# A second V pair kept across two attention layers, parked in four PSUM banks, with a guarded return

## The chip, the cores and the metric

The kernel runs on one core of one Trainium2 chip. The metric is the device time of one execution in microseconds; it is about 1.7 us longer than the span from the first to the last instruction that the profile shows. Before the change the median of four runs measured with it was 187.67 us (187.57 to 188.01). A profile is one execution: that of the changed kernel was the slowest of its four (186.12 us), and those of "late_return", "deep_return" and "two_slots" were the slowest of theirs.

## The reference, cut to what matters

Four sub-layers act on a batch of four single tokens, in bf16: attention, a gated linear unit (GLU), the same attention again, the same GLU again. Weights and caches are the same both times.

```python
x = x + _A_ref(_layernorm(x), K, V, wq, wo)             # attention
x = x + _B_ref(_layernorm(x), w_gate, w_up, w_down)     # GLU
x = x + _A_ref(_layernorm(x), K, V, wq, wo)             # the same K, V, wq, wo
x = x + _B_ref(_layernorm(x), w_gate, w_up, w_down)
# attention: 4 sequences, 8 KV heads, 32 query heads of 128, the last 2048 positions
# D = 512, F = 1792
```

A K or V "pair" below is one KV head of two of the four sequences: 1 MiB, 8 KB per partition. There are 16 pairs of K and 16 of V.

## The kernel before

SBUF holds an arena of 50 slots of 4 KB per partition. K takes 32 of them and stays for both attentions. The other 18 are nine places of one pair each: wo takes four for both attentions, one V pair is kept from the first attention to the second, and about four places float. Everything else (V, wq, the GLU weights) streams through those and is read a second time for the second layer. The sync engine (SP) issues the loads in one order; each waits until the last reader of its place is done. So a place that frees late delays the load that will take it and every load after it.

```python
KEEP_V = cfg.get("KEEP_V", 1)
SB = (0, 1); PBS = (2, 3); OBS = (4, 5); WB = 6; CB = 7      # PSUM banks
...
def load_v(h, bp, k, n_use):
    load(("V", h, bp, k), n_use, "bw_8k", (2 * SLOT, pair_d(A_v, h, bp), True))
...
def q_proj(k, b0, b1):
    for n, i in enumerate((0, 1) if k == 0 else (1, 0)):     # two halves of q
        qb = OBS[n]
        for c in range(NC):
            ...                                              # 4 matmuls of 512 columns each
            P.op("tensor", "q%d_%d_%d" % (k, i, c), ..., r=tok(s) + [("xn",)], w=[("qrow", i)], banks=(qb,))
            done(name)                                       # frees the wq place after its last reader
        P.op("vector", "qt%d_%d" % (k, i), ...)              # transpose
        P.op("vector", "qc%d_%d" % (k, i), ...)              # scale
        P.op("tensor", "qs%d_%d" % (k, i), ...)              # spread over the partitions
        P.op("scalar", "qp%d_%d" % (k, i), ...)
...
all_v = [(h, bp) for h in range(HKV) for bp in range(2)]
keep = all_v[len(all_v) - KEEP_V:]
...                                                          # loads of the first attention
load_glu(0)
load_wq(1)
for h in range(HKV)[::-1]:                                   # second attention, heads 7 to 0
    for bp in range(2)[::-1]:
        if (h, bp) not in keep:
            load_v(h, bp, 1, 1)
load_glu(1)
```

A scheduler orders the operations of each engine from their dependences. "S2.0" and "S2.1" are the first two score blocks of the second attention.

Of the kernel before, what the change touches and what calls it, by code (L numbers as in the profile page):

```python
# [6 lines left out]
F32 = mybir.dt.float32  # L7
# [265 lines left out]
def build(nc, A_x, A_k, A_v, A_wq, A_wo, B_wg, B_wu, B_wd, out, cfg=None):  # L273
    cfg = dict(cfg or {})
# [1 line left out]
    tm.update(cfg.get("tm", {}))  # L276
    NS = cfg.get("NS", 50)
    GROUPS = cfg.get("GROUPS", [[0, 1, 2, 3]])
    KEEP_V = cfg.get("KEEP_V", 1)
    NG = len(GROUPS)  # L280
    assert GROUPS == [[0, 1, 2, 3]]
    N_DMA_SEMS = cfg.get("N_DMA_SEMS", 24)
# [32 lines left out]
    with es:  # L315
# [161 lines left out]
        def load_glu(k):  # L477
# [3 lines left out]
            for (a, b) in bounds_of(k):  # L481
                load(("wd", a, k), 1, "bw_8k", ((b - a) * D, wd_d[:, a:b, :], False))

        def load_v(h, bp, k, n_use):
            load(("V", h, bp, k), n_use, "bw_8k", (2 * SLOT, pair_d(A_v, h, bp), True))

# [101 lines left out]

        def q_proj(k, b0, b1):
            assert b0 == 0 and b1 == NB  # L590
            for n, i in enumerate((0, 1) if k == 0 else (1, 0)):
                qb = OBS[n]
                for c in range(NC):
                    name, o = wq_part(k, c, i)
                    s = need(name)

                    def e_q(pe, c=c, s=s, qb=qb, o=o):
                        last = None
                        for hh in range(4):
                            last = pe.matmul(ps[32 * hh:32 * hh + NB, qb, :], xn[:, c * NB:(c + 1) * NB],  # L600
                                             tile_ap(s)[:, o + hh * 512:o + (hh + 1) * 512],
                                             start=(c == 0), stop=(c == NC - 1))
                        return last
                    P.op("tensor", "q%d_%d_%d" % (k, i, c), 4 * tm["pe_row"], e_q,
                         r=tok(s) + [("xn",)], w=[("qrow", i)], banks=(qb,))
                    done(name)
                P.op("vector", "qt%d_%d" % (k, i), c_dve(512),
                     lambda v, qb=qb: v.transpose(  # L608
                         ebuf[:, :], ps[:, qb, :].rearrange("p (x k t) -> p x t k", k=32, t=2)),
                     r=[("qrow", i)], w=[("e", 0), ("e", 1)], banks=(qb,))  # L610
                qi = qh[:, i * 64:(i + 1) * 64]
                P.op("vector", "qc%d_%d" % (k, i), c_dve(64),
                     lambda v, qi=qi: v.tensor_scalar(
                         qi.rearrange("p (b c r) -> p b c r", c=4, r=REP),
                         ebuf[:, :].rearrange("p (r c y) -> p y c r", c=4, y=32)[:, 0:NB], SCALE, None, ALU.mult),
                     r=[("e", 0), ("e", 1)], w=[("qh", i)])

                def e_rep(pe, qi=qi):
                    last = None
                    for hh in range(4):  # L620
                        for a in range(4):
                            last = pe.matmul(ps[32 * a:32 * a + 32, CB, hh * 64:(hh + 1) * 64],
                                             ident_b[:, 32 * hh:32 * hh + 32], qi, start=True, stop=True)
                    return last
                P.op("tensor", "qs%d_%d" % (k, i), 300.0, e_rep, r=[("qh", i), ("ident_b",)],
                     w=[("cb",)], banks=(CB,))
                P.op("scalar", "qp%d_%d" % (k, i), c_act(256),
                     lambda a, i=i: a.copy(qrep[:, i * 256:(i + 1) * 256], ps[:, CB, 0:256]),  # L628
                     r=[("cb",)], w=[("qrep", i)], banks=(CB,))
# [144 lines left out]
        def attn(L):  # L774
            hs = list(range(HKV)) if L == 0 else list(range(HKV))[::-1]

            def front(ui):
                h = hs[ui]
                if L == 0:
                    k_transpose(h)  # L780
                k2 = softmax_unit("%d.%d" % (L, ui), h)
                if L == 2:
                    for bp in range(2):
                        pool.release(4 * h + 2 * bp)
                    fill()
                return k2

            ks = {}
            for ui in range(2):
                ks[ui] = front(ui)  # L790
                turn_p("%d.%d" % (L, ui), ks[ui])
            for ui, h in enumerate(hs):
                tag = "%d.%d" % (L, ui)
                if ui + 2 < HKV:
                    ks[ui + 2] = front(ui + 2)
                ov = pv_unit(tag, h, ks[ui], v_tiles[(L, h)])
                if ui + 2 < HKV:
                    turn_p("%d.%d" % (L, ui + 2), ks[ui + 2])
                wo_unit(tag, h, ov, ks[ui], ui == 0, ui == HKV - 1)
            P.op("vector", "xa%d" % L, tm["dve_fix"] + 40.0,  # L800
                 lambda v: v.tensor_tensor(xT[:, 0:NX], ps[:, WB, 0:NX], xT[:, 0:NX], ALU.add),
                 r=[("psw",)] + [("xT", b) for b in range(NB)], w=[("xT", b) for b in range(NB)], banks=(WB,))

        def glu(k, b0, b1, last=False):
# [7 lines left out]
            for n, nm in enumerate(("wg", "wu")):  # L812
                for c in range(NC):
                    name = (nm, c // 2, k)
                    s = need(name)

                    def e_g(pe, c=c, s=s, n=n):
                        last = None
                        for g in range(4):
                            o = c % 2 * F + g * NF  # L820
                            last = pe.matmul(ps[32 * g:32 * g + NB, SB[n], 0:NF], xn[:, c * NB:(c + 1) * NB],  # L821
                                             tile_ap(s)[:, o:o + NF], start=(c == 0), stop=(c == NC - 1))
                        return last
                    P.op("tensor", "gl%s%d_%d" % (nm, k, c), 4 * tm["pe_row"], e_g,
                         r=tok(s) + [("xn",)], w=[("gu", n)], banks=(SB[n],))
                    done(name)
                P.op("vector", "gt%s%d" % (nm, k), c_dve(NF),
                     lambda v, n=n: v.transpose(ebuf[:, 0:NF],  # L828
                                                ps[:, SB[n], 0:NF].rearrange("p (x k) -> p k x", k=NFC)),
                     r=[("gu", n)], w=[("e", 0), ("e", 1)], banks=(SB[n],))  # L830

                if n == 0:
                    P.op("scalar", "gex%d" % k, c_act(NH),
# [79 lines left out]

        all_v = [(h, bp) for h in range(HKV) for bp in range(2)]
        keep = all_v[len(all_v) - KEEP_V:]
        load_wq(0)
        for h in range(2):
            loads.append((("K", h), lambda _, h=h: load_k(h)))
# [6 lines left out]
                load_v(h, bp, 0, 2 if (h, bp) in keep else 1)  # L925
        load_glu(0)
        load_wq(1)
        v_tiles = {}
        for h in range(HKV)[::-1]:
            v_tiles[(0, h)] = [(bp, ("V", h, bp, 0)) for bp in range(2)]  # L930
            v_tiles[(2, h)] = [(bp, ("V", h, bp, 0 if (h, bp) in keep else 1)) for bp in range(2)[::-1]]
            for bp in range(2)[::-1]:
                if (h, bp) not in keep:
                    load_v(h, bp, 1, 1)
# [82 lines left out]
```

## Time and profile before

| | before |
|---|---|
| span of the profile | 186.2 us |
| HBM read | 72.88 MB |
| V loads of 1 MiB | 31 |
| DVE busy | 84.5 us |
| landing of the last load (second w_down) | 182.69 us |
| tail from there to the end | 3.53 us |

These are lines of the profile page of the kernel before: the clock granted to PE, the busy share of the 16 DMA engines and the rate, in 40 equal slices of the span; then the bytes; then the chain of waits that ended last, by engine.

```profile
span 186.2 us, 4414 instructions
...
PEclk9999997685857558576576555555796969955587
DMA  5999999999999999999999999999999999999970
GB/s 191 424 424 431 424 402 388 415 422 417 405 392 422 417 422 400 396 422 419 388 408 414 406 402 390 362 400 419 422 419 419 415 419 421 417 412 404 413 318 15
...
HBM read 72.88 MB, written 0.00 MB: 391 GB/s over the span
...
DMA 54%; PE 24%; SPq 14%; DVE 3%; ACT 2%; issue 2%; POOL 0%
```

The DMA row is at 9 nearly throughout, 54% of the chain is DMA, and the fullest slices run at 419 to 431 GB/s.

The next view is the table of windows for the start of the second attention. Columns: window, its length, then for each engine busy us and instructions, then PE's granted clock, the mean DMA load in units of 16 engines, and GB/s.

```profile
129.00:131.50 2.50, 2.50 (x28) 0.82 (x28) 0.62 (x3) 0.86 (x4) 0.00 (x0) 0.50 1.02 423
131.50:134.00 2.50, 1.98 (x22) 0.55 (x16) 2.09 (x7) 1.16 (x5) 0.03 (x1) 0.68 1.01 423
134.00:136.50 2.50, 2.50 (x39) 1.02 (x39) 1.40 (x8) 1.54 (x4) 0.99 (x5) 1.00 1.01 419
```

The stream runs at 419 to 423 GB/s there. By the landings of single loads, the V loads that land there follow each other by 2.48 to 2.49 us.

The timeline of DVE (the vector engine) around the end of the first attention and around the first half of q (start us, us, engine, line, operation, output and input; in brackets how long the engine was idle before, and what ended that):

```profile
107.32 0.20 DVE L749 TENSOR_TENSOR onb<-ps,rinv 128x16 bf16<-128x16 f32 x1 [4.79 <-PE ps L741]
...
126.55 0.72 DVE L608 STREAM_TRANSPOSE ebuf<-ps 128x512 f32<-128x512 f32 x1 [3.58 <-PE ps L600]
```

DVE is idle for 4.79 us before 107.32, which is room for four transposes. Second, SP's timeline between 128.5 and 134 us, which shows how many V loads were issued in that window:

```profile
129.09 4.93 SPq L382 DMA_DIRECT2D arena<-in_A_v_cache_dram  x2
```

Two: one at 129.09, the other ending at 134.02. Third, PE's timeline at the start of the second attention (L668 are the score blocks S2.0 and S2.1, L600 the last eight products of q):

```profile
128.99 3.84 PE L668 MATMUL ps<-arena,qbd 128*16 128x512 bf16 x32
132.59 0.86 PE L600 MATMUL ps<-arena,xn 128*4 128x512 bf16 x8
```

### The profile page before, as it was taken

The numbers are of one execution on the slowest core, as the hardware profiler recorded it, in microseconds if no ns is written. First come the engines' busy times: TensorE is split into PE (matmuls) and PEld (weight loads), VectorE is DVE, ScalarE is ACT, GpSimd is POOL, SyncE is SP. The second block draws the span as 40 slices with busy tenths as digits, with TensorE's granted clock in tenths as the row PEclk, the third lists the DMA queues.
The fourth block names the chain that finished last, engine by engine and source line by source line (L and its number), as shares of the span: only waits on it lengthen the run. The fifth ranks groups of instructions, "written<-read, shape, count | busy, mean of one in ns | idle before, by whom it ended". The sixth has DMA issues, their size and how long they took to land.

```text
span 186.2 us, 4414 instructions
## 1 busy us (share of the span) xinstructions
PE 101.8 (55%) x1944; PEld 55.3 (30%) x1944; DVE 84.5 (45%) x213; ACT 35.9 (19%) x100; POOL 14.9 (8%) x77
## 2 busy tenths in 40 slices
PE   0532423743616346252464545337899899947545
PEld 0101000332302223032233430311256565547112
DVE  5209998476582656727430031213754343312210
ACT  2003022330303003020020001002564332310100
POOL 4000010110101001010010000000121101120000
PEclk9999997685857558576576555555796969955587
DMA  5999999999999999999999999999999999999970
GB/s 191 424 424 431 424 402 388 415 422 417 405 392 422 417 422 400 396 422 419 388 408 414 406 402 390 362 400 419 422 419 419 415 419 421 417 412 404 413 318 15
DMA packets 15523, 73.17 MB, mean 393 GB/s; under 512 B 1160, under 2 KB 5264, under 8 KB 8720
## 3 DMA queue, kind: packets, MB, share of 16 engines
q1 hardware_dynamic: 15496, 72.88, 97.1%
q8 instruction: 15, 0.25, 0.5%
q14 instruction: 4, 0.03, 0.0%
q10 hardware_dynamic: 8, 0.00, 0.0%
HBM read 72.88 MB, written 0.00 MB: 391 GB/s over the span
## 4 chain that ended last, share of the span: by engine, by line
DMA 54%; PE 24%; SPq 14%; DVE 3%; ACT 2%; issue 2%; POOL 0%
DMA arena<-in_A_v_cache_dram 36%; SPq L382 14%; DMA arena<-in_B_w_down_dram 14%; PE ps L668 11%; PE ps L741 6%; DMA arena<-in_A_wq_dram 5%; PE ps L874 2%; PE ps L765 1%; ACT prow L685 1%; PE ps L697 1%; DVE nmax L676 1%; PE ps L898 1%; PE ps L720 1%; PE ps L600 1%; PE ps L821 1%
## 5 line engine op out<-in xcount | busy, mean ns | idle before, releaser
L741 PE MATMUL ps<-ebuf,arena 128*128 128x8 bf16 x1024 | 30.8, 167 | 30.8 <-DMA arena<-in_A_v_cache_dram 27.3
L668 PE MATMUL ps<-arena,qbd 128*16 128x512 bf16 x256 | 32.2, 628 | 15.7 <-DVE qbd L639 8.2
L741 PEld LDWEIGHTS ps<-ebuf,arena 128*128 128x128 bf16 x1024 | 28.6, 100 | 37.4 <-DMA arena<-in_A_v_cache_dram 33.4
L649 DVE STREAM_TRANSPOSE arena<-arena 128x1024 f32<-128x1024 f32 x32 | 37.9, 1218 | 3.6 <-DMA arena<-in_A_k_cache_dram 3.3
L676 DVE TENSOR_REDUCE nmax<-ps 128x1 f32<-128x512 f32 x16 | 11.0, 686 | 23.7 <-PE ps L668 23.7
L685 ACT ACTIVATE prow<-ps,nmax 128x512 bf16<-128x512 f32 x16 | 11.0, 687 | 37.9 <-DVE nmax L682 25.2
L642 ACT COPY qbd<-qrep 32x64 bf16<-32x64 bf16 x32 | 7.7, 242 | 41.2 <-PE ps L668 40.7
L668 PEld LDWEIGHTS ps<-arena,qbd 128*16 128x16 bf16 x256 | 6.4, 98 | 30.3 <-issue 21.6
L749 DVE TENSOR_TENSOR onb<-ps,rinv 128x16 bf16<-128x16 f32 x16 | 3.0, 186 | 26.5 <-PE ps L741 26.4
L710 POOL CAST s<-psm 128x1 bf16<-128x1 f32 x16 | 3.0, 188 | 143.2 <-ACT prow L685 143.2
L600 PE MATMUL ps<-arena,xn 128*4 128x512 bf16 x64 | 8.0, 596 | 7.3 <-DMA arena<-in_A_wq_dram 4.4
L702 ACT CAST prow<-ps 128x512 bf16<-128x512 f32 x16 | 9.4, 588 | 7.1 <-PE ps L697 7.0
L765 PE MATMUL ps<-onb,arena 128*128 128x4 bf16 x256 | 9.0, 165 | 3.1 <-DVE onb L749 3.1
L706 DVE STREAM_TRANSPOSE ebuf<-prow 128x256 f32<-128x256 f32 x16 | 7.0, 440 | 7.3 <-ACT prow L702 7.1
L821 PE MATMUL ps<-arena,xn 128*4 128x448 bf16 x64 | 6.6, 536 | 5.7 <-DVE xn L582 3.1
L765 PEld LDWEIGHTS ps<-onb,arena 128*128 128x128 bf16 x256 | 7.9, 100 | 3.7 <-DVE onb L749 2.8
L697 PE MATMUL ps<-prow,perm 64*128 64x256 bf16 x64 | 6.7, 291 | 2.3 <-ACT prow L685 2.1
L608 DVE STREAM_TRANSPOSE ebuf<-ps 128x512 f32<-128x512 f32 x4 | 2.9, 717 | 10.6 <-PE ps L600 10.5
L571 ACT ACTIVATE lnv<-lnv 128x4 f32<-128x4 f32 x4 | 0.8, 205 | 34.1 <-DVE lnv L568 34.1
L828 DVE STREAM_TRANSPOSE ebuf<-ps 128x448 f32<-128x448 f32 x4 | 2.6, 650 | 9.5 <-PE ps L821 9.5
L639 DVE COPY qbd<-qrep 32x64 bf16<-32x64 bf16 x32 | 5.3, 165 | 1.5 <-ACT qrep L628 0.9
L720 PE MATMUL ps<-sel_b,s 128*128 128x16 bf16 x48 | 3.8, 176 | 3.4 <-POOL s L714 2.6
(59 smaller groups left out, 65.1 us busy)
## 6 DMA issues: line engine op xcount, KB each, us to landing
arena<-in_A_v_cache_dram SPq DMA_DIRECT2D x31, 1024.0 KB, 17.0
arena<-in_A_k_cache_dram SPq DMA_DIRECT2D x16, 1024.0 KB, 16.1
arena<-in_A_wq_dram SPq DMA_DIRECT2D x8, 1024.0 KB, 9.1
arena<-in_A_wo_dram SPq DMA_DIRECT2D x4, 1024.0 KB, 24.3
arena<-in_B_w_gate_dram SPq DMA_DIRECT2D x4, 896.0 KB, 19.8
arena<-in_B_w_up_dram SPq DMA_DIRECT2D x4, 896.0 KB, 16.1
arena<-in_B_w_down_dram SPq DMA_DIRECT2D x2, 1024.0 KB, 12.7
arena<-in_B_w_down_dram SPq DMA_DIRECT2D x1, 768.0 KB, 6.9
```

Of the source, the lines that this page charges most:

```text
L382: o = P.op("sync", name, 0.0, lambda e, dst=dst, src=src: e.dma_start(dst, src), r=r, w=w, dma_bytes=nbytes, dma_rate=tm[rate])
L600: last = pe.matmul(ps[32 * hh:32 * hh + NB, qb, :], xn[:, c * NB:(c + 1) * NB], tile_ap(s)[:, o + hh * 512:o + (hh + 1) * 512], start=(c = ...
L642: P.op("scalar", "qe%s_%d" % (tag, a), c_act(64), lambda s_, dst=dst, src=src: s_.copy(dst, src), r=rd, w=[("q", k2, a)])
L649: P.op("vector", "T%d_%d" % (h, t), c_dve(1024), lambda v, v32=v32: v.transpose(v32, v32), r=[("slot", 4 * h + t)], w=[("slot", 4 * h + t)])
L668: last = pe.matmul(ps[32 * gi:32 * gi + NR, bank, :], qbd[:, q0:q0 + NR], kt[:, cp // 2, cp % 2, b % 2, :, :], start=(cp == 0), stop=(cp = ...
L676: lambda v: v.tensor_reduce(nmax[:, k2:k2 + 1], ps[:, bank, :], AXX, ALU.max),
L685: lambda a: a.activation(prow[:, :].rearrange("p (m x t) -> p m x t", x=16, t=2), ps[:, bank, :].rearrange("p (m t x) -> p m x t", x=16, t ...
L697: last = pe.matmul(ps[:, PBS[i], 0:256], perm[64 * i:64 * i + 64, jh * 128:(jh + 1) * 128], prow[64 * i:64 * i + 64, jh * 256:(jh + 1) * 2 ...
L702: lambda a: a.copy(prow[:, :].rearrange("p (y i t) -> p i y t", i=2, t=2), ps[:, PBS[0]:PBS[0] + 2, 0:256].rearrange("p i (y t) -> p i y t ...
L741: last = pe.matmul(ps[:, ob, bp * 8:bp * 8 + 8], src[:, j * 128:(j + 1) * 128], ev[:, j % 2, j % 16 // 2, x0:x0 + 8], start=(j == 0), stop ...
L765: last = pe.matmul(ps[:, WB, c * NB:(c + 1) * NB], tile_ap(s)[:, o + r_ * D + c * 128:o + r_ * D + (c + 1) * 128], ov[:, r_ * NB:(r_ + 1) ...
L821: last = pe.matmul(ps[32 * g:32 * g + NB, SB[n], 0:NF], xn[:, c * NB:(c + 1) * NB], tile_ap(s)[:, o:o + NF], start=(c == 0), stop=(c == NC ...
```

## The change

The intent is to keep a second V pair, V(head 7, pair 0), so that its second 1 MiB read is never made. The arena of 50 slots has no place to spare, so at the end of the first attention DVE moves the pair into PSUM banks 0 to 3 with four transposes ("st"), and moves it back into a freed SBUF place with four more ("us") when the second attention needs it. Transposing twice is meant to restore every bit. The kernel declares its PSUM tensor as 128 x 8 x 512 f32, so one of the eight bank numbers stands for 2 KB per partition, and four hold exactly the 8 KB per partition of a pair.

The banks must not be used in between, so gate and up products move from SB to OBS. Two guards order the return: the fourth transpose back waits for the scaling of the first half of q ("qc"), and the second half of q waits until the first half is spread ("qs"). The diff, cut (index changes of the GLU banks shortened):

```diff
-    KEEP_V = cfg.get("KEEP_V", 1)
+    KEEP_V = cfg.get("KEEP_V", 2)
...
+        STASH = SB + PBS
+        after_q = []
+        def stash(name):
+            s = need(name)
+            for n, b in enumerate(STASH):
+                src = tile_ap(s)[:, n * 1024:(n + 1) * 1024].bitcast(F32)
+                P.op("vector", "st%d" % n, ..., lambda v, src=src, b=b: v.transpose(ps[:, b, :], src),
+                     r=tok(s), w=[("stash", n)], banks=(b,))
+            done(name)
+        def load_stash(name):
+            left[name] = 1
+            def emit(s):
+                for n, b in enumerate(STASH):
+                    dst = tile_ap(s)[:, n * 1024:(n + 1) * 1024].bitcast(F32)
+                    o = P.op("vector", "us%d" % n, ..., lambda v, dst=dst, b=b: v.transpose(dst, ps[:, b, :]),
+                             r=[("stash", n)], w=[("slot", s + n // 2)], banks=(b,))
+                    o.prio += 60
+                    if n == 3:
+                        after_q.append(o)
+            loads.append((name, emit))
...
 # q_proj
+            qs = []
-                         r=tok(s) + [("xn",)], w=[("qrow", i)], banks=(qb,))
+                         r=tok(s) + [("xn",)], w=[("qrow", i)], banks=(qb,), after=qs if k else ())
...
+                while after_q:
+                    after_q.pop().deps.add(qc)
...
+                qs.append(qs_)
...
 # attention, after the last score block of the first layer
+                if L == 0 and ui == HKV - 1:
+                    stash(stashed)
...
 # GLU: gate and up products in OBS[n] instead of SB[n]
...
 # list of loads of the second layer
         load_wq(1)
+        load_stash(("V",) + keep[0] + (1,))
```

One thing moves that the diff does not spell out. Of the 16 products of q's second half, the first eight run ahead of S2.0 in both kernels. Before, PE ran S2.1 ahead of the last eight; after, the scheduler puts these between S2.0 and S2.1. PE's timeline after (L697 are the score blocks, L626 the products of q):

```profile
129.15 2.01 PE L697 MATMUL ps<-arena,qbd 128*16 128x512 bf16 x16
130.94 0.66 PE L626 MATMUL ps<-arena,xn 128*4 128x512 bf16 x8
131.39 2.09 PE L697 MATMUL ps<-arena,qbd 128*16 128x512 bf16 x16
```

More of the change, by code (lines that the diff above doesn't have):

```diff
@@ L482, in load_glu @@
                 load(("wd", a, k), 1, "bw_8k", ((b - a) * D, wd_d[:, a:b, :], False))
+        STASH = SB + PBS
[4 more added lines that the diff above has]
+                src = tile_ap(s)[:, n * 1024:(n + 1) * 1024].bitcast(F32)
+                P.op("vector", "st%d" % n, c_dve(512), lambda v, src=src, b=b: v.transpose(ps[:, b, :], src),
+                     r=tok(s), w=[("stash", n)], banks=(b,))
[5 more added lines that the diff above has]
+                    dst = tile_ap(s)[:, n * 1024:(n + 1) * 1024].bitcast(F32)
+                    o = P.op("vector", "us%d" % n, c_dve(512), lambda v, dst=dst, b=b: v.transpose(dst, ps[:, b, :]),
+                             r=[("stash", n)], w=[("slot", s + n // 2)], banks=(b,))
[3 more added lines that the diff above has]
+            loads.append((name, emit))
         def load_v(h, bp, k, n_use):
@@ L611, in q_proj @@
                 qi = qh[:, i * 64:(i + 1) * 64]
-                P.op("vector", "qc%d_%d" % (k, i), c_dve(64),
+                qc = P.op("vector", "qc%d_%d" % (k, i), c_dve(64),
                      lambda v, qi=qi: v.tensor_scalar(
@@ L624, in e_rep @@
                     return last
-                P.op("tensor", "qs%d_%d" % (k, i), 300.0, e_rep, r=[("qh", i), ("ident_b",)],
+                qs_ = P.op("tensor", "qs%d_%d" % (k, i), 300.0, e_rep, r=[("qh", i), ("ident_b",)],
                      w=[("cb",)], banks=(CB,))
+                qs.append(qs_)
                 P.op("scalar", "qp%d_%d" % (k, i), c_act(256),
@@ L820, in e_g @@
                             o = c % 2 * F + g * NF
-                            last = pe.matmul(ps[32 * g:32 * g + NB, SB[n], 0:NF], xn[:, c * NB:(c + 1) * NB],
+                            last = pe.matmul(ps[32 * g:32 * g + NB, OBS[n], 0:NF], xn[:, c * NB:(c + 1) * NB],
                                              tile_ap(s)[:, o:o + NF], start=(c == 0), stop=(c == NC - 1))
@@ L824, in glu @@
                     P.op("tensor", "gl%s%d_%d" % (nm, k, c), 4 * tm["pe_row"], e_g,
-                         r=tok(s) + [("xn",)], w=[("gu", n)], banks=(SB[n],))
+                         r=tok(s) + [("xn",)], w=[("gu", n)], banks=(OBS[n],))
                     done(name)
@@ L828, in glu @@
                      lambda v, n=n: v.transpose(ebuf[:, 0:NF],
-                                                ps[:, SB[n], 0:NF].rearrange("p (x k) -> p k x", k=NFC)),
-                     r=[("gu", n)], w=[("e", 0), ("e", 1)], banks=(SB[n],))
+                                                ps[:, OBS[n], 0:NF].rearrange("p (x k) -> p k x", k=NFC)),
+                     r=[("gu", n)], w=[("e", 0), ("e", 1)], banks=(OBS[n],))
                 if n == 0:
@@ L915, in build @@
         keep = all_v[len(all_v) - KEEP_V:]
+        stashed = ("V",) + keep[0] + (0,)
         load_wq(0)
@@ L930, in build @@
             v_tiles[(0, h)] = [(bp, ("V", h, bp, 0)) for bp in range(2)]
-            v_tiles[(2, h)] = [(bp, ("V", h, bp, 0 if (h, bp) in keep else 1)) for bp in range(2)[::-1]]
+            v_tiles[(2, h)] = [(bp, ("V", h, bp, 0 if (h, bp) in keep[1:] else 1)) for bp in range(2)[::-1]]
             for bp in range(2)[::-1]:
```

## The prediction

> **What bounds the kernel now.** The input stream. The page shows 72.88 MB read and the DMA row at 9 tenths in all but the first and the last two slices. In the chain that ended last DMA has 54%, waits before issues 14%, PE 24%. [...] the table of windows shows 419 GB/s for 129 to 161 us[...]. By each load's landing in the trace, consecutive 1 MiB V loads land 2.48 to 2.50 us apart. After the last w_down piece (182.69 us) 3.5 us of tail remain.
>
> **What the change does.**
> - It removes one 1 MiB load, the second read of V(head 7, pair 0): issued at 124.19 us, landed at 133.23 us, 2.48 us after the load before. Estimate: 2.48 us of stream.
> - It adds eight 512-element DVE transposes. Estimate 0.6 to 0.72 us each (0.72 us measured out of a PSUM bank; 1.22 us for 1024 elements in place), 5.5 us in all; DVE is 45% busy.
> - The four going out fit between that pair's landing (103.72 us) and DVE's next work at 107.32 us: estimate 103.8 to 106.7 us. They hold back the second w_up load from 104.8 to about 106.7 us, with 6 us of earlier loads still to land (7.8 now): nothing lost.
> - Of the four coming back, three start when two q products end (124.15 us) and take to 126.4 us; the q transpose starts at 126.55 us now and slips by 0 to 0.2 us. The fourth runs while PE and ScalarE spread q (127.6 to 128.4 us).
> - Gate and up products only change banks. PE puts the second half of q between the first two score blocks, so the second block's softmax comes about 1 us later. That attention is compute-paced to about 161 us, but the loads behind it land last: off the path.
>
> **Does the stream stay full?** The returned pair takes a free slot that a load would have had. At the issues of V(6,1), V(6,0), V(5,1) the stream today has 6.0 to 6.2 us left to land; I expect 3.1 to 3.7. The smallest backlog today is 2.96 us (first w_down piece, 112.2 us); 106 to 129 us ran at 394 GB/s. So a loss of 0 to 0.4 us is possible, no drained queue. After 134 us score blocks free the K slots and the queue is deep again.
>
> **How much is on the path.** Everything after the removed load lands 2.5 us earlier: last landing near 180.2 us, the same tail. 187.68 - 2.48 + 0.1 = 185.3 us, 1.3% faster, inside the 2% band. Range 184.7 to 186.4. Chances: faster by over 2% 0.03, within 2% 0.95, slower by over 2% 0.02.
>
> **What the profile would show.** HBM read 71.83 MB; 30 V loads, not 31; DMA row still at 9; DVE busy about 90 us; landings as before up to the last wq load (130.75 us, within 0.3 us); the first score block of the second layer near 129 us, at most 0.3 us late; the last landing 2.5 us earlier, then the same 3.5 us; a w_down landing still the chain's last DMA piece.
>
> **What would make it wrong.** A bubble of 1 us or more in the stream between 130 and 140 us from the thinner backlog; transposes into PSUM slower than 0.9 us, so that the end of the first attention, and the layer change with it, slips; slow packets on wq or V loads falling differently; a lower granted PE clock that delays slot releases.

## The result

| | before | after |
|---|---|---|
| time, median of 4 runs (range) | 187.67 us (187.57 to 188.01) | 185.49 us (185.17 to 186.12) |
| span of the profile | 186.2 us | 184.4 us |
| HBM read | 72.88 MB | 71.83 MB |
| V loads | 31 | 30 |
| DVE busy | 84.5 us | 89.5 us |
| last landing | 182.69 us | 181.75 us |
| tail after it | 3.53 us | 2.64 us |

The ratio is 0.9885 (95% interval 0.9855 to 0.9915). All ratios here are the mean time of one kernel's runs over that of the other's of the same rounds, so not quite the ratio of the medians quoted. Executions over 1.5% slower than the fastest of the same kernel are left out of the means. The changed kernel is 1.15% faster, inside the 2% band, and its time is within 0.2 us of the prediction. But the last two rows are not what the prediction said: the last landing came only 0.94 us earlier, and the tail shrank.

The same lines of the page, after:

```profile
span 184.4 us, 4421 instructions
...
PEclk9999995585766756755555555555897897885569
DMA  5999999999999999999999999999999999999980
GB/s 198 425 427 427 425 403 391 411 421 419 409 387 425 419 421 403 392 419 419 400 391 414 412 407 393 403 350 417 330 396 419 419 423 416 418 416 402 412 341 24
...
HBM read 71.83 MB, written 0.00 MB: 390 GB/s over the span
...
DMA 52%; PE 25%; SPq 16%; DVE 4%; issue 2%; ACT 0%
```

The DMA row still says 9, yet the rate has two holes, 350 and 330 GB/s. A slice is 184.4/40 = 4.6 us. The first hole is the slice from 120 us, in the wq loads; the kernel before has one there too (362). The second, from 129 to 134 us, is new: that part of the page before has 419 and more. The table of windows, cut finer, tells better:

```profile
129.00:131.50 2.50, 2.50 (x32) 0.89 (x32) 0.63 (x3) 0.84 (x5) 0.00 (x0) 0.72 1.12 349
131.50:134.00 2.50, 2.16 (x38) 0.82 (x30) 2.06 (x7) 1.13 (x4) 0.06 (x1) 1.00 0.87 321
134.00:136.50 2.50, 2.34 (x23) 0.51 (x23) 1.51 (x7) 1.22 (x4) 0.70 (x4) 1.00 1.01 370
```

Beside 423, 423 and 419 GB/s before. In the first window the engines were busier than usual (1.12) and moved less. The packets explain that: an 8 KB packet usually takes 311 ns, and between 128.8 and 136.3 us 18 of them took 1.0 to 2.03 us. A stalled packet counts as a busy engine in this view (a share of 1.12 at 349 GB/s, against 1.02 at 423 before), so the rate shows the loss and the share does not.

DVE's timeline, after:

```profile
103.59 2.50 DVE L492 STREAM_TRANSPOSE ps<-arena 128x512 f32<-128x512 f32 x4 [1.21 <-DMA arena<-in_A_v_cache_dram]
107.16 0.19 DVE L778 TENSOR_TENSOR onb<-ps,rinv 128x16 bf16<-128x16 f32 x1 [1.06 <-PE ps L770]
...
124.18 1.91 DVE L502 STREAM_TRANSPOSE arena<-ps 128x512 f32<-128x512 f32 x3 [1.34 <-PE ps L626]
126.70 0.72 DVE L634 STREAM_TRANSPOSE ebuf<-ps 128x512 f32<-128x512 f32 x1 [0.61 <-PE ps L626]
127.45 0.22 DVE L639 TENSOR_SCALAR qh<-ebuf 128x64 bf16<-128x64 f32 x1
127.71 0.72 DVE L502 STREAM_TRANSPOSE arena<-ps 128x512 f32<-128x512 f32 x1
```

The moves are as planned: about 0.62 us each going out, in the idle time at 103.6 to 106.1, with DVE's next operation even a little earlier (107.16 against 107.32); three back, then the q transpose 0.15 us later than before (126.70 against 126.55), and the fourth right after the scaling. DVE was idle before the first two groups and again before its next work, so none of its own work waits for them in this view.

SP, in the same window as before:

```profile
129.23 4.91 SPq L382 DMA_DIRECT2D arena<-in_A_v_cache_dram  x5
```

Five issues instead of two. One of them is V(5,1), that is head 5, pair 1, which was issued at 133.49 before and at 131.65 after, because the last products of q run before S2.1 and the wq place is free earlier: they end at 133.45 before and 131.60 after, each time 0.05 us before the issue.

### Where the 1.83 us of the profile came from

The last landing alone misleads. The trace keeps 16 semaphore increments at different times for each load of the stream. The author read each as the landing of one DMA engine's share, since the page counts 16 engines; the trace does not name the engine, so "the slowest engine" below means the last of a load's 16 increments. Read so, each load has 16 landings; their spread over a load grows here from 1.50 us (before) and 1.76 (after) at the last wq load to 2.88 and 3.29 at the end. Three numbers add up to the span: the mean of the 16 landings of the last w_down load, how far the slowest engine is behind that mean (lag), and the tail after it.

| us | mean landing | lag | tail | sum = span |
|---|---|---|---|---|
| before | 181.25 | 1.44 | 3.53 | 186.22 |
| after | 179.79 | 1.97 | 2.64 | 184.39 (sum 184.40) |
| change | -1.46 | +0.53 | -0.89 | -1.83 |

So of about 2.5 us of stream that were removed, 1.46 reached the mean landing, the slowest engine gave back 0.53, and a shorter tail added 0.89.

A second measure isolates the stretch of V loads: from the mean landing of the last wq load to that of the last V load. Before, 15 loads took 37.83 us, 2.522 each. In "after", 14 loads should take 35.31 and took 36.50: 1.2 us lost. This is the "loss" in the tables below.

### The tail

PE's timeline at the end; the products with w_down are L874 before and L905 after.

```profile
180.86 3.15 PE L874 MATMUL ps<-arena,hT 128*4 128x256 bf16 x28 [1.93 <-DMA arena<-in_B_w_down_dram]
```

```profile
179.93 1.04 PE L905 MATMUL ps<-arena,hT 128*4 128x256 bf16 x16 [1.09 <-DMA arena<-in_B_w_down_dram]
181.17 1.01 PE L905 MATMUL ps<-arena,hT 128*4 128x256 bf16 x12 [0.20 <-DMA arena<-in_B_w_down_dram]
```

Before, 28 products took 3.15 us without a gap: at half clock, PE could not keep up with the pieces of w_down as they landed. After, they took 2.05 us and PE waited for the pieces. The windows just before and during them, before and then after:

```profile
177.50:180.90 3.40, 0.83 (x14) 0.15 (x12) 0.87 (x2) 0.00 (x0) 0.00 (x0) 0.99 0.83 333
180.90:184.30 3.40, 3.11 (x28) 1.63 (x28) 0.25 (x1) 0.25 (x1) 0.00 (x0) 0.50 0.13 51
```

```profile
174.70:178.20 3.50, 2.84 (x32) 1.10 (x33) 0.82 (x2) 0.43 (x3) 0.00 (x0) 0.50 1.01 408
178.20:181.60 3.40, 2.12 (x36) 1.16 (x31) 0.87 (x2) 0.34 (x2) 0.00 (x0) 1.00 0.33 130
```

The column before the DMA share is the clock: 0.50 during the products before, 1.00 after. In the clock records of the two traces it is either 1.00 or 0.50, and every entry but the last lasts 3.41 us or a multiple of it. In this pair of windows the lower clock came after the lesser PE work: before, the window with PE busy for 0.83 us was followed by half clock; after, the one with 2.84 by full clock. But PE's busy time does not decide it alone. With the records of these two traces cut into steps of 3.41 us, a step in which PE was busy for less than 1.25 us was followed by half clock in 25 of 25 cases, and one at half clock with over 3.25 us busy by full clock in 8 of 8; yet after 3 of 9 steps at full clock with over 3.25 us busy the clock fell to half. What decides there, no run tests.

### The profile page after: what moved, and what is told of

Read it like the earlier page. It is cut to its first block, busy times and chain, and to the rows that moved or that the text cites. A ratio compares the mean times of both kernels' runs of the same rounds, so it can differ in the third digit from the quotient of the medians.

```text
span 184.4 us, 4421 instructions
## 1 busy us (share of the span) xinstructions
PE 101.2 (55%) x1944; PEld 54.7 (30%) x1944; DVE 89.5 (49%) x221; ACT 35.7 (19%) x100; POOL 14.8 (8%) x77
## 3 DMA queue, kind: packets, MB, share of 16 engines
HBM read 71.83 MB, written 0.00 MB: 390 GB/s over the span
## 4 chain that ended last, share of the span: by engine, by line
DMA 52%; PE 25%; SPq 16%; DVE 4%; issue 2%; ACT 0%
DMA arena<-in_A_v_cache_dram 33%; SPq L382 16%; PE ps L697 11%; DMA arena<-in_B_w_down_dram 9%; PE ps L770 8%; DMA arena<-in_A_wq_dram 5%; DMA arena<-in_B_w_up_dram 5%; PE ps L726 2%; PE ps L794 1%; DVE ps L492 1%; PE ps L626 1%; DVE nmax L705 1%; PE ps L749 1%; PE ps L905 1%; PE ps L852 1%
## 5 line engine op out<-in xcount | busy, mean ns | idle before, releaser
L697 PE MATMUL ps<-arena,qbd 128*16 128x512 bf16 x256 | 32.5, 626 | 16.9 <-DVE qbd L668 8.4
L697 PEld LDWEIGHTS ps<-arena,qbd 128*16 128x16 bf16 x256 | 6.1, 97 | 31.3 <-issue 22.0
L626 PE MATMUL ps<-arena,xn 128*4 128x512 bf16 x64 | 7.8, 582 | 7.6 <-DMA arena<-in_A_wq_dram 6.2
L726 PE MATMUL ps<-prow,perm 64*128 64x256 bf16 x64 | 7.4, 315 | 2.4 <-ACT prow L714 2.3
```

Of the source, the lines that this page charges most:

```text
L626: last = pe.matmul(ps[32 * hh:32 * hh + NB, qb, :], xn[:, c * NB:(c + 1) * NB], tile_ap(s)[:, o + hh * 512:o + (hh + 1) * 512], start=(c = ...
L697: last = pe.matmul(ps[32 * gi:32 * gi + NR, bank, :], qbd[:, q0:q0 + NR], kt[:, cp // 2, cp % 2, b % 2, :, :], start=(cp == 0), stop=(cp = ...
L726: last = pe.matmul(ps[:, PBS[i], 0:256], perm[64 * i:64 * i + 64, jh * 128:(jh + 1) * 128], prow[64 * i:64 * i + 64, jh * 256:(jh + 1) * 2 ...
```

## The experiments

Three theories were to be told apart. A: the gain is the bytes, and the stalls in a thin stream are their price. B: the DVE work, the moved banks or the new PE order make the difference. C: part of the gain is a tail that the clock decides.

### The changed kernel and the kernel before, once more

Neither is edited.

> The changed kernel once more, unedited, as the control of this group. In its first trace only 0.94 us of the 2.48 us reached the last landing: between 126 and 140 us packets that took over 1.15 times the usual time of their size cost 23.6 engine-us, 1.47 us on each of 16 engines (1.55 engine-us in the kernel before). Theory 'thin stream' (with two loads still under way, engines run short of queued packets and stall): the same cluster at the same place, excess 10 to 30 engine-us, time about 185.4 us. Rival 'accident of that one run': no cluster, excess under 5 engine-us, last landing 2.3 us or more earlier than before, that is at or below 180.4 us.

185.49 us (184.77 to 186.57, six runs) against 187.69: 0.9884 (0.9853 to 0.9916). The result repeats. Mean landing 179.35, lag 1.89, tail 2.63; loss 0.6 us. So the stall is there again but half as long (an excess of 12.1 where 10 to 30 were expected), and the short tail is there again.

> The kernel before once more, unedited, for a second trace of it. In the first trace the 16 engines' shares of the last load landed at 181.25 us on average and at 182.69 us for the slowest (1.44 us behind the average), and 3.53 us of tail followed with the TensorE clock granted at half while the down products ran. If these are properties of the kernel: average 181.0 to 181.5 us, slowest 1.2 to 1.7 us behind it, slow packets at 126 to 140 us under 5 engine-us, tail 3.4 to 3.9 us. If they are accidents of one run, they differ by more than that.

One run, 187.44 us, profile 185.71: mean 181.31 and lag 1.48, as in the first profile (181.25 and 1.44), but a tail of 2.91. The first 16 products with w_down took 1.04 us there, at full clock. So the stream of the kernel before is steady, and its tail varies with the clock.

### The bytes alone

On the kernel before: the second read of V(7,0) fetches 512 bytes per partition instead of 8 KB, into the same place with the same waits. The data are wrong, though the deviation stayed within the comparison's tolerance.

```diff
 def load_v(h, bp, k, n_use):
+    if (h, bp, k) == (7, 0, 1):
+        load(("V", h, bp, k), n_use, "bw_8k", (256, pair_d(A_v, h, bp)[:, :, 0:256], True))
+        return
```

> The kernel before with the second load of V(head 7, pair 0) cut to 512 B a partition (64 KB); the slot, the order of all instructions and all waits stay; the result is wrong on purpose. No transposes to or from PSUM, no moved banks, but the same thin stream: V(6,1) is issued at 126.5 us with about 3.6 us of earlier loads left to land. Theory 'thin stream': slow packets at 128 to 136 us as in the changed kernel, excess 10 to 30 engine-us, time 185.3 to 185.9 us. Rival 'the transposes or the new order of PE cause the slow stretch': excess under 5 engine-us and 2.3 us faster than before, about 185.3 us.

187.86 us against 187.69: 1.0007 (0.9973 to 1.0042). All but 64 KB of the 1 MiB is gone and nothing is gained. The slow packets came as expected, the expected time (185.3 to 185.9) did not, and neither did that of the rival. This was the most telling result. The windows and SP's timeline of this run:

```profile
129.00:131.50 2.50, 2.50 (x28) 0.84 (x24) 0.01 (x1) 0.19 (x2) 0.00 (x0) 0.50 1.02 391
131.50:134.00 2.50, 2.19 (x24) 0.66 (x16) 2.08 (x7) 1.14 (x4) 0.00 (x0) 0.80 0.96 377
134.00:136.50 2.50, 2.09 (x20) 0.60 (x24) 1.66 (x7) 1.74 (x5) 0.81 (x4) 1.00 0.78 239
```

```profile
129.65 4.62 SPq L382 DMA_DIRECT2D arena<-in_A_v_cache_dram  x2
```

With PE's old order V(5,1) is issued at 133.74 us, when by the landings only 2.48 us of earlier loads were left and one load was outstanding. The rate falls to 239 GB/s, and V(5,1) lands 4.98 us after the load before it instead of 2.5. The loss of the V stretch is 1.8 us (37.28 us for 14 1/16 loads), and the lag grows to 1.90. Here the stream loses in two ways. Slow packets cost 17.2/16 = 1.1 us per engine, and for another 0.9 us, by the start and end of all packets, the engines had nothing to do: the DMA share falls to 0.78. In "after" there was next to no such idle time (0.03 us), only slow packets. Theory A in its plain form falls: with V(5,1) issued as late as 133.74 us, the bytes taken out were worth nothing (1.0007).

### DVE work and PE order alone

On the changed kernel: all bytes are read again. The pair's second load goes into the place, and the four transposes back run in place in PSUM.

```diff
 # load_stash, emit
+    held = [x for t_ in tok(s) for x in P.readers.get(t_, [])]
+    dma(str(name), tile_ap(s), pair_d(A_v, name[1], name[2]), w=tok(s), rate="bw_8k")
-    ... lambda v, dst=dst, b=b: v.transpose(dst, ps[:, b, :]), r=[("stash", n)], w=[("slot", s + n // 2)]
+    ... lambda v, b=b: v.transpose(ps[:, b, :], ps[:, b, :]), r=[("stash", n)], w=[("stash", n)], after=held
```

> The changed kernel with the second load of V(head 7, pair 0) kept: the pair still goes to PSUM (four transposes), the four return transposes run at the same place but write their own bank in place, and the slot is filled by the load; banks and order of PE as changed. If the eight transposes, the moved banks and the new order are free: 187.7 us as before, within 0.3 us, and no slow stretch at 126 to 140 us (excess under 5 engine-us, as the stream is as deep as before). Rival 'the added work costs time': 188.2 us or more, or slow packets at 128 to 136 us with the deep stream.

187.54 us against 187.69: 0.9989 (0.9969 to 1.0008). Eight transposes, the moved banks and the new PE order, tested together, cost nothing measurable and gain nothing with all bytes in the stream. V(5,1) is issued at 131.21 instead of 133.49, and that changes nothing: the stream had 6.23 us left there. B alone falls.

### The bytes and the PE order, without any stash

On "bytes_only": the second score block waits for the last product of q's second half, as the scheduler orders it in the changed kernel.

```diff
 # softmax_unit
-    w=[("pss", k2)], banks=(bank,))
+    w=[("pss", k2)], banks=(bank,), after=[x for x in P.ops if tag == "2.1" and x.name == "q1_0_3"])
```

> The run 'bytes_only' (second load of V(head 7, pair 0) cut to 64 KB, no transposes, wrong on purpose), which was no faster than the kernel before, with one edit: the second score block waits for the second half of q, so PE has the order of the changed kernel. In 'bytes_only' the load of V(5,1) was issued at 133.7 us with 2.5 us of earlier loads left and landed 5.0 us after the load before it, 2.5 us late; in the changed kernel it is issued at 131.6 us. Theory 'the order of PE carries the gain': V(5,1) issued near 131.6 us, its step under 4 us, time 185.0 to 186.2 us. Rival 'cutting the load saves nothing in itself, the transposes or their timing did it': 187.3 us or more.

186.44 us (184.51 to 186.59) against 187.81: 0.9904 (0.987 to 0.9938). One dependence turns no gain into most of the gain. SP's timeline:

```profile
128.75 5.46 SPq L382 DMA_DIRECT2D arena<-in_A_v_cache_dram  x5
```

V(5,1) goes out at 131.73 with 4.05 us left; the loss falls from 1.8 to 0.5 us. The profiled run had the long tail (3.51, half clock) and a lag of 2.29. So removing the bytes alone is worth nothing, moving the last products of q forward is worth nothing with the bytes kept ("dve_only", together with the DVE work), and both are worth about 1% together.

### Without the two guards

On the changed kernel:

```diff
-    ..., banks=(qb,), after=qs if k else ())
+    ..., banks=(qb,))
...
-                while after_q:
-                    after_q.pop().deps.add(qc)
```

> The changed kernel without the two waits: the fourth return transpose does not wait for the first half's q, and the second half of q does not wait for the spreading of the first. By the order of instructions the fourth transpose then stands between the q transpose and the scaling of q on DVE, and two products of the second half stand before the spreading of q on PE. The spreading of q should come 0.7 to 1.3 us later and the first score block with it. Theory 'PE is just under the stream in the second attention' (in the changed kernel PE ends the second attention 2 us after the last V load landed): about that much slower, 185.9 to 186.8 us. Rival 'PE has slack there': 185.5 us, as the changed kernel.

186.84 us (186.02 to 188.59) against 187.81: 0.9962 (0.9921 to 1.0003). By the means the guards are worth about 0.8% (0.9962 against 0.9884, though from different groups of runs, each with its own runs of before). S2.0 starts at 130.14 us instead of 129.15, V(5,1) goes out at 132.98 with 2.81 us left and lands 5.35 us after its predecessor; the loss is 1.5 us and the lag 3.64. The last products of q stand before S2.1 here too, but the spreading of q now stands behind eight products of the second half (128.70 us instead of 127.73), and S2.0 and the last products of q come later with it. So the guards keep PE's order such that the wq place frees early. This profile was one of the slower runs (188.16 us).

### Both pairs in SBUF

On the kernel before: KEEP_V = 2 and nothing else. Both pairs hold SBUF places; PSUM is not used.

```diff
-    KEEP_V = cfg.get("KEEP_V", 1)
+    KEEP_V = cfg.get("KEEP_V", 2)
```

> The kernel before with two pairs kept, both in SBUF slots, no PSUM: the same 1 MiB saved, but one slot fewer for loads over the whole change of layers. Theory 'thin stream': the loads of w_down, wq and the first V pairs are issued one release later, with 2 to 4 us left each time; more slow packets between 106 and 140 us than in the changed kernel, and 186.5 to 189 us. Rival 'the slot does not matter, only bytes do': 185.2 to 185.7 us, as the changed kernel.

188.19 us (four runs, 187.52 to 189.96) against 187.81: 1.0009 (0.9981 to 1.0038). The same 1 MiB is saved and nothing is gained. The profile fell on the slowest of these runs, so its span (188.21) is not typical, but it shows where the place is missed. PE's timeline in the first GLU:

```profile
116.50 0.92 PE L821 MATMUL ps<-arena,xn 128*4 128x448 bf16 x8 [2.70 <-DMA arena<-in_B_w_up_dram]
```

The second w_up load was issued at 111.76 us, with 0.71 us of stream left; before it was issued at 104.81 with 7.76 left. PE waited 2.70 us for it. So PSUM matters as a place that is not taken from the stream.

### A later return

On the changed kernel: the returned pair takes its place after V(6,0) in the order of loads, so that two loads go out before it and the stream is fuller.

```diff
         load_wq(1)
-        load_stash(("V",) + keep[0] + (1,))
 ...
             for bp in range(2)[::-1]:
                 if (h, bp) not in keep:
                     load_v(h, bp, 1, 1)
+                    if (h, bp) == (6, 0):
+                        load_stash(("V",) + keep[0] + (1,))
```

> The changed kernel with the return of the stashed pair moved two places back in the list of loads, after V(6,1) and V(6,0). These two loads get the slots of the first four q products and are issued at about 124.2 and 126.7 us instead of 126.7 and 129.2, so the stream has some 6 us left to land at both, as before the change; V(5,1) comes at about 131.7 us with 3.5 us left. The return transposes then run at 129.2 us, and the first score block starts some 0.7 us later. Theory 'thin stream': excess at 126 to 140 us falls from 23.6 to under 8 engine-us, last landing near 180.4 us, time 184.7 to 185.2 us, faster than the changed kernel. Rival 'these V loads are slow behind wq by their addresses': the cluster stays, 10 engine-us or more.

186.43 us against 187.69: 0.9929 (0.9909 to 0.9949), slower than the changed kernel, although the stream is better: last landing 180.00 us, 1.2 us before that of "after_again" (181.23). The gain went to a new wait. PE's timeline, then DVE's:

```profile
129.81 1.93 PE L697 MATMUL ps<-arena,qbd 128*16 128x512 bf16 x16 [1.06 <-DVE arena L502]
```

```profile
128.94 1.91 DVE L502 STREAM_TRANSPOSE arena<-ps 128x512 f32<-128x512 f32 x3
```

The first score block waits 1.06 us for a bank that the return is still emptying, so it starts at 129.81 against 129.15. PE remains late: its last block of P·V products begins at 171.97 against 170.46, and the tail grows to 5.15 us. The mean clock of that profile was also lower (0.677 against 0.703), so how much of the 1.5 us comes from the wait of 0.66 is open. It does show that in the changed kernel PE is only a little ahead of being the limit itself. The rival of the expectation, that these loads are slow by their addresses, was not settled: the excess of 9.4 lies between the 8 and the 10 that were named for the two.

### A later return in other banks

This combines both lessons. On "late_return": the pair lies in banks 1, 2, 3 and 4, so that the first score block's bank is free; the GLU and q of the second layer use banks 0 and 5 instead of 4 and 5; three transposes of the return come after DVE's inputs of the second score block, the fourth after the maximum of the first, and S2.1 after the second half of q.

```diff
-        STASH = SB + PBS
+        STASH = (SB[1],) + PBS + (OBS[0],)
+        GBS = (SB[0], OBS[1])                       # for q of the second layer, gate and up
...
+    st:   after=[x for x in P.ops if x.name == "oe0.6"]
+    us0..2: after qe2.1_2;  us3: after nm2.0;  S2.1: after q1_0_3;  no o.prio += 60
```

> A version meant to be better: return of the stashed pair after V(6,1) and V(6,0) as in 'late_return', but the pair is stashed in the banks 1 to 4, so that the first score block (bank 0) does not wait for the return, whose transposes stand behind the spreading of q on DVE; second half of q before the second score block. 'late_return' had the stream complete 1.2 us earlier than the changed kernel (180.0 us) but PE 1.9 us later, and took 186.4 us. If both readings hold: V(6,1), V(6,0) and V(5,1) issued at 124.2, 126.7 and 131.7 us, first score block near 129.1 us, last landing 179.8 to 180.5 us, time 184.0 to 185.0 us. If PE stays the later one: 185.3 us or more with the last landing near 180 us.

186.25 us (184.18 to 186.88) against 187.81: 0.9903 (0.9864 to 0.9942): no better than the changed kernel, and short of the 184.0 to 185.0 that was hoped for. It had the smallest loss of the runs without the load so far (0.3 us) and the earliest mean landing (178.63), and S2.0 starts at 128.61. But the slowest of the 16 engines was 3.03 us behind, and the tail was 3.50 at half clock.

### The clock of the tail

Ten filler matmuls (128x512, into a bank that is free then) keep PE busy before the w_down products: four before the gate products, two after the residual's row products, four after the up products.

```diff
+    warm("wmA", 4, ("ln_sumG1", "xa2"), ("glwg1_0",))
+    warm("wmB", 2, ("xrow",), ("glwu1_2",))
+    wmc = warm("wmC", 4, ("glwu1_3",), ())
...                                                  # xrow placed after glwu1_1
-    r=tok(s) + [("hT",)], w=[("orow",)], banks=PBS)
+    r=tok(s) + [("hT",)], w=[("orow",)], banks=PBS, after=[wmc])
```

> The kernel before with ten filler matmuls (128 x 512, into a free PSUM bank, results unused) in PE's idle gaps of the last gate and up products: four behind the layer norm's sum, two before the last up products, four before the down products. Theory 'the tail is shorter in the changed kernel only because the clock is granted in full when PE had no gaps just before': down products in 2.0 to 2.3 us instead of 3.15, tail 2.5 to 2.8 us instead of 3.5, time 186.6 to 187.1 us, all without any change to the loads. Rival 'the tail depends on when the loads land': tail 3.4 us or more, 187.7 us.

On the kernel before: 187.16 us against 187.83, 0.9961 (0.9935 to 0.9987). The products:

```profile
181.00 1.04 PE L891 MATMUL ps<-arena,hT 128*4 128x256 bf16 x16 [0.81 <-DMA arena<-in_B_w_down_dram]
182.23 1.02 PE L891 MATMUL ps<-arena,hT 128*4 128x256 bf16 x12 [0.20 <-DMA arena<-in_B_w_down_dram]
```

Full clock and a tail of 2.64 us, as in the changed kernel, with the stream of the kernel before (mean 181.34, lag 1.48). This confirms that the clock makes the difference between the two tails; over the timed runs it was worth 0.4%, less than the 0.9 us of the first profile, as unedited runs have full clock there at least some of the time ("before_again" did for 16 of the 28 products).

> The changed kernel with the same ten fillers. Its tail was 2.6 us in three of three traces, so the fillers should change little: 184.9 to 185.6 us, tail 2.4 to 2.8 us, if the clock is the cause and the changed kernel has it in most runs; about 0.3 us faster than the changed kernel if some of its runs have the slow clock, with less spread. Slower than 185.8 us would mean that the fillers delay the products.

On the changed kernel: 187.04 us against 187.83, 0.9955 (0.9916 to 0.9995). Worse than without. The fillers before the gate products came in the way: three of the four ran only from 173.53 us, and the gate products followed them at 174.92, 3.5 us after the layer norm's products where "after" has 2.3. The tail of 3.19 explains about 0.6 us of the 1.3 us that the ratios differ by; the rest is open.

> 'deep_return' (pair in banks 1 to 4, return behind two V loads) with the same ten fillers. Its shares of the last load landed at 178.63 us on average, 1.16 us before those of the changed kernel, but its slowest engine was 3.0 us behind and its tail 3.5 us at the half clock. Theory 'three separate terms: stream, slowest engine, clock': average 178.4 to 179.2 us, tail 2.4 to 2.8 us, time 184.2 to 185.4 us depending on the slowest engine (1.5 to 3 us behind). Rival 'the version is no better in itself': 186 us or more.

On "deep_return": 186.89 us against 187.83, 0.9947 (0.9915 to 0.998). Here the stream had no stall at all (loss 0.1 us, excess 2.4) although the load is removed and only 3.39 us were left at V(5,1), it ended best of all timed versions but one (last landing 180.36), and PE ended late (tail 4.59). No version that was tried beats the changed kernel.

### All runs side by side

"Left" is the time that earlier loads still had to land when V(5,1) was issued (issue times are the start of the issuing instruction, "left" is counted from its end), "excess" the time that packets took beyond their usual time between 126 and 140 us, summed over the 16 engines (packets of over 1.15 times the usual time for their size). Mean and lag are of the last load. Ratios are to the runs of before of the same group.

| run | V(5,1) issued | left | excess | loss | mean | lag | tail | ratio |
|---|---|---|---|---|---|---|---|---|
| before | 133.49 | 4.18 | 1.6 | 0 | 181.25 | 1.44 | 3.53 | |
| before_again | 133.92 | 4.06 | 2.6 | 0.0 | 181.31 | 1.48 | 2.91 | |
| before_warm | 133.50 | 4.30 | 1.4 | 0.0 | 181.34 | 1.48 | 2.64 | 0.9961 |
| dve_only | 131.21 | 6.23 | 1.8 | 0.0 | 180.85 | 1.34 | 3.85 | 0.9989 |
| bytes_only | 133.74 | 2.48 | 17.2 | 1.8 | 180.43 | 1.90 | 3.55 | 1.0007 |
| bytes_order | 131.73 | 4.05 | 7.4 | 0.5 | 179.03 | 2.29 | 3.51 | 0.9904 |
| after | 131.65 | 4.89 | 23.6 | 1.2 | 179.79 | 1.97 | 2.64 | 0.9885 |
| after_again | 131.63 | 4.30 | 12.1 | 0.6 | 179.35 | 1.89 | 2.63 | 0.9884 |
| unguarded | 132.98 | 2.81 | 21.6 | 1.5 | 180.16 | 3.64 | 2.62 | 0.9962 |
| late_return | 132.64 | 2.76 | 9.4 | 0.5 | 179.12 | 0.88 | 5.15 | 0.9929 |
| deep_return | 131.71 | 3.31 | 8.5 | 0.3 | 178.63 | 3.03 | 3.50 | 0.9903 |
| two_slots | 135.19 | 2.74 | 17.8 | 1.6 | 181.51 | 3.21 | 3.49 | 1.0009 |
| after_warm | 132.03 | 4.49 | 13.2 | 1.0 | 179.75 | 1.93 | 3.19 | 0.9955 |
| deep_warm | 131.83 | 3.39 | 2.4 | 0.1 | 178.95 | 1.42 | 4.59 | 0.9947 |

The four traces that keep all bytes have no stall to speak of (excess up to 2.6); of the ten with the load removed, nine have one (7.4 to 23.6), and "deep_warm" has none. The "left" at this one load does not decide it alone: "late_return" had only 2.76 us left there but had issued the two loads before it with over 6 us left, and lost little, while "after" issued all three with 3.5 to 4.9 us left and lost the most time to slow packets. The kernel before had 4.18 us left here and lost nothing. So slow packets go with a thin stream in these traces, but a thin stream does not bring them each time, and no figure of "left" parts the cases; why a packet then takes 1 to 2 us is not shown.

## Why the prediction was right, and where it was not

The total, the class and the range held. Step by step:

- **Bound by the stream, and the load is worth 2.48 us of it.** Right as a value: at the pace of before a V load is worth 2.5 us. But not right as a term that can be taken off by itself. "bytes_only" removes it and gains nothing.
- **Transposes: 0.6 to 0.72 us, hidden.** Right: 0.62 going out, 0.64 to 0.72 coming back, DVE at 89.5 us (about 90 predicted), and "dve_only" at 0.9989 says that they cost nothing.
- **w_up held back to about 106.7 us with nothing lost.** Right: issued at 106.19 with 6.25 us left, landing at 115.02 against 115.15.
- **First score block near 129, at most 0.3 late; landings up to the last wq load as before.** Right: 129.15 against 128.99, and 130.74 against 130.75.
- **"Off the path" for PE's new order.** Wrong. The sentence looked at the second block's softmax, which does come later. It missed that the same move frees a wq place about 2 us earlier. "bytes_only" against "bytes_order" measures that: 1.0007 against 0.9904.
- **"Does the stream stay full?": a loss of 0 to 0.4 us.** This is the step that failed most. 3.50 us left at the first of the three issues was as predicted (3.1 to 3.7); 4.86 and 4.89 at the next two are more because earlier loads were already landing late. The loss was 1.2 us in "after" and 0.6 in "after_again". The argument that 2.96 us were survived at 112.2 us before did not carry over; why is not tested. And the base was misread: the kernel before had 6.15 and 6.09 us left at V(6,1) and V(6,0), but only 4.18 at V(5,1), not 6.0 to 6.2. With the old order of PE about 4.2 - 2.5 = 1.7 us would have remained there by this account ("bytes_only" measured 2.48, as its loads landed late as well). That it was 4.89 in "after" is in good part owed to the move which the prediction called off the path, so this was luck. The third point of "what would make it wrong" and the first together describe what happened.
- **DMA row still at 9.** It is, and it could not have told: in the window with stalled packets the engines' share was 1.12 at 349 GB/s. The GB/s row shows the holes (350 and 330).
- **Last landing 2.5 us earlier.** Wrong: 0.94 us in that profile, 1.46 in "after_again" (182.69 to 181.23). Besides the stall, the slowest engine's lag grew by 0.5 us.
- **The same tail.** Wrong: 2.64 instead of 3.53, by the clock. The prediction listed a lower clock as a danger for slot releases; a higher one at the end was not thought of.

So two steps were wrong in opposite directions. In the terms of the profile, the removed load gave -2.5, the stall +1.2, an earlier start of the stretch -0.2 (the last wq load's mean landing was 129.73 instead of 129.89), the lag +0.5, the tail -0.9: together -1.9 by rounded terms, -1.83 measured, where the prediction had -2.4. The median over the runs fell by 2.2 us, between the two profiles (-1.83 and, for "after_again", -2.36). In the profiled run the short tail made up for most of the stall, and that was luck; how much of either is in the median of 185.49, which the figure 185.3 met, the timed runs do not show.

What stays open: how much of the spread of the changed kernel (184.77 to 186.57 us over six runs, wider than that of before) is the clock in the tail and how much the slowest engine, as only profiled runs show either. Three profiles with the changed kernel's order at the end (after, after_again, unguarded) had the short tail, but "dve_only" with the same order there had 3.85 at half clock, and of the two of before one had part of it (3.53 and 2.91). So the short tail is not shown to be a property of the change. Which of the 16 engines falls behind, and why, the trace does not tell.

## What to carry to other kernels

In this kernel, which a stream of loads bounds, the removed load was worth its time only when the next load could be issued earlier. Elsewhere, look at which instruction frees its place, and at how much of the stream is left at that moment. Look at GB/s, not at busy DMA engines alone, to see a stream that starves: in "after" the DMA row stayed at 9 in the slice that moved 330 GB/s. And judge a profile's gain in terms (mean landing, slowest engine, tail with its clock), since opposite errors in two terms can make a total look well understood.

## What else the traces show

- With 2.48 to 4.89 us left to land at V(5,1), nine of the ten traces with the load removed lost 0.3 to 1.8 us of stream, and in "after" 8 KB packets took up to 2.03 us instead of 311 ns. In the kernel before, with 6.2, 6.1 and 4.2 us left at V(6,1), V(6,0) and V(5,1), nothing was lost, and in "deep_warm" (6.0, 5.9 and 3.4) 0.1 us.
- The landings of one load drift apart: 1.50 us (before) and 1.76 (after) at the last wq load, 2.88 and 3.29 at the last load of all. Over all 14 traces the last landing of the last load came 0.88 to 3.64 us behind the mean.
- The tail at full clock instead of half was 0.89 us shorter, of a span of 186.2 us; that is about half of the 1.83 us by which the two profiles differ.
- In each of the two profiles PE has one gap of over 1 us that no semaphore ended. It lies inside the P·V products and lasts 2.41 us before and 2.43 after. A 16 KB read on the queue that the page calls "instruction" starts within 0.05 us of the start of the gap (at 164.81 us before, where the gap begins at 164.84; at 166.02 after, where it begins at 165.98). The kernel before has 14 more such reads without such a gap. The lines before and after are below; that the read causes the gap was not tested.

```profile
167.25 1.78 PE L741 MATMUL ps<-ebuf,arena 128*128 128x8 bf16 x61 [2.41 <-issue]
```

```profile
168.41 1.77 PE L770 MATMUL ps<-ebuf,arena 128*128 128x8 bf16 x61 [2.43 <-issue]
```
